# Bringing the second batch's first head pair forward into the first batch's last, with its loads between smaller groups of weight columns

## The chip, the cores and the metric

The kernel runs on one core of a Trainium2 chip. The metric is device time in microseconds (us), lower is better. The median of the kernel before is 318.94 us over its first three runs (318.9 to 319.49). The runs of the kernel before spread by 0.2% to 1.2% within one batch (318.9 to 319.49 us in the first, 316.93 to 320.62 in the last), and its medians moved from 318.9 to 319.7 us between batches, so every experiment below is read by its ratio to runs of the kernel before on the same chip in the same rounds.

Names: PE is the matmul engine (TensorE), PEld its weight load, DVE is VectorE, ACT is ScalarE, POOL is GpSimd, SP issues most loads. PSUM holds the tiles that PE writes in the traces below (psTk, psGT, psS, psH). T(4) and S(4,0) stand for what `emit_T(4)` and `emit_S(4, 0)` make.

## The reference, cut to what matters

Eight batches, eight heads of width 64, 512 local and 32 global positions. The attention output goes through a gated feed-forward product.

```python
# local queries see 32 neighbours on each side and all 32 global keys
# global queries see everything; softmax over each row
x = attn_out.transpose(0, 2, 1, 3).reshape(B * S, H * D)     # 8 * 544 rows of 512
h = x @ w_in                                                 # 512 -> 2048
g = h * np.clip(h + 3.0, 0.0, 6.0) / 6.0
out = g @ w_out                                              # 2048 -> 512
```

## The kernel before

The work is cut into 32 head pairs, four to a batch. Pairs 0 to 3 are batch 0, pairs 4 to 7 batch 1. For each pair `emit_T` transposes k and q on PE, `emit_S` makes two halves of the scores and their exponentials, `emit_AV` multiplies by v, and `emit_X` transposes the result for the feed-forward product. `u1(c)` makes one block of 128 of the 2048 columns of `x @ w_in`, in four matmuls (one for each pair of the batch), followed by one activation on ScalarE and one gate product on VectorE. In the traces below each engine makes its matmuls, copies and activations in the order in which the program emits them (on ScalarE in the kernel before: the casts of w_in 4 to 7 end at 24.47 us, the activations of the first seven blocks start at 24.63, the copy of qT(4) at 28.64, the exponentials of S(4,0) at 31.69; PE's and VectorE's timelines are below).

```python
def load_w(kind, i):            # one 256 KB tile of w_in, float32, into a staging buffer
    nc.sync.dma_start(out=t, in_=moe_w_in[m * P:(m + 1) * P, qd * 512:(qd + 1) * 512])
def cast_w(kind, i, eng):       # to float16, on the engine that is given
    (eng.copy if eng is nc.scalar else eng.tensor_copy)(out=o, in_=w_st[kind, i])
...
def emit_T(p, qdve=False):
    ...                          # 8 transposes on PE
    nc.vector.tensor_copy(out=kv[...], in_=ps["k"]...)       # kT on VectorE, L229
    qcopy(out=qT[...], in_=ps["q"]...)                       # qT on ScalarE, L232
    ...                          # and its first 32 columns once more, L237
def cast_G(b0, b1, nm, eng=nc.vector):                       # global keys to float16, VectorE, L191
def emit_G(b0, b1, nm):          # transposes them on PE (L201), copies to kgT on VectorE (L209)
def kglob(b, eng):               # copies kgT into kT, L213; the second half of the scores reads it
def vglob(b, eng):               # copies the global values into vb, L147; 1.88 us on GpSimd
def emit_S(p, ch):
    ...                          # 2 matmuls that write the mask (L281), 8 of scores (L293),
    ...                          # 2 exponentials on ScalarE (L297)
def u1(c, ms=range(NM)):
    ...                          # 4 matmuls, L426
    nc.scalar.activation(out=t1[:, 0:n], in_=ps[:, 0:n], func=RELU, ...)          # L431
    nc.vector.scalar_tensor_tensor(out=gts[c][:, 0:n], in0=t1[:, 0:n], ...)       # L433
```

The order of compute around the seam between the batches:

```python
    emit_S(3, 1)
    for i in range(4, 8):
        cast_w("in", i, nc.scalar)          # four casts on ScalarE
    emit_X(1)
    emit_AV(2)
    HEAD = 4
    for c in range(HEAD):
        u1(c, range(2))                      # pairs 0 and 1 of the first four blocks
    emit_X(2)
    emit_AV(3)
    for c in range(HEAD):
        u1(c, range(2, 3))
    emit_X(3)
    for c in range(HEAD):
        u1(c, range(3, 4))
    u1(4)
    u1(5)
    u1(6)
    emit_T(4)
    cast_G(1, 4, "kg")
    emit_T(5)
    emit_G(1, 4, "kg")
    emit_S(4, 0)
    u1(7)
    kglob(1, nc.vector)
    u1(8)
    emit_S(4, 1)
    ...
```

The softmax here doesn't subtract the row's maximum and nothing guards it: scores larger than these inputs give would overflow.

Of the kernel before, what the change touches and what calls it, by code (L numbers as in the profile page):

```python
# [14 lines left out]
def kernel(  # L15
# [12 lines left out]
    nc = tc.nc  # L28
# [88 lines left out]
    def load(p, what="kqv"):  # L117
        b, m = divmod(p, NM)
        s = st.setdefault(p, {})
        for c in what:  # L120
            src = {"k": k_l, "q": q_l, "v": v_l}[c]
            t = stage()
            if c != "v" and b < NRUN:
                nc.sync.dma_start(out=t.rearrange("p (h x) -> p h x", h=2),  # L124
                                  in_=src[b, 2 * m:2 * m + 2].rearrange("h (p j) d -> p h (j d)", j=NT))
            else:
                nc.sync.dma_start(out=t.rearrange("p (h kb d) -> p (h kb) d", h=2, kb=NT),  # L127
                                  in_=src[b, 2 * m:2 * m + 2].rearrange("h (kb p) d -> p (h kb) d", p=P))
            s[c + "f"] = t.rearrange("p (h kb d) -> p kb h d", h=2, kb=NT)

    def cast(p, what, eng):
        b, m = divmod(p, NM)
        s = st[p]
        for c in what:
            if c == "v":
                o = vts[b % NV][:, :, m, vc].rearrange("p kb (h d) -> p kb h d", h=2)
            else:
                s[c + "n"] = wrk.tile([P, NT, P], FP16, tag=c + "n", name=c + "n", bufs=4)
                o = s[c + "n"].rearrange("p kb (h d) -> p kb h d", h=2)
            eng.tensor_copy(out=o, in_=s[c + "f"])  # L140
# [27 lines left out]
    def cast_w(kind, i, eng):  # L168
        if kind == "in":
            qd, m = divmod(i, NM)  # L170
            o = w_in_t[m][:, qd * 512:(qd + 1) * 512]
        else:
            o = w_out_t[i // 4][:, i % 4]
        (eng.copy if eng is nc.scalar else eng.tensor_copy)(out=o, in_=w_st[kind, i])  # L174
# [5 lines left out]
    def load_g(b0, b1, nm):  # L180
        src = {"kg": k_g, "qg": q_g}[nm]
        t = stage()
        nc.sync.dma_start(
            out=t[:, 0:(b1 - b0) * HH * D].rearrange("p (n d) -> p n d", d=D),
            in_=src[b0:b1].rearrange("b (x y) s d -> (y s) (b x) d", x=HH))
        gst[b0, nm] = t
# [29 lines left out]
    def emit_T(p, qdve=False):  # L216
        b, m = divmod(p, NM)
        s = st[p]
        kT = kTs[b % 2][:, m]
        kv = kT[:, 0:NT * KW].rearrange("p (u c) -> p u c", u=NT)  # L220
        qT = wrk.tile([P, Sl + W], FP16, tag="qT", name="qT", bufs=5)
        ps = {}
        for c in "kq":
            ps[c] = ps_tile("psT" + c, FP16)[:, 0:Sl]
            for j in range(NT):
                nc.tensor.matmul(out=ps[c][:, j * P:(j + 1) * P], lhsT=s[c + "n"][:, j], rhs=ident,
                                 is_transpose=True)
        qcopy = nc.vector.tensor_copy if qdve else nc.scalar.copy
        nc.vector.tensor_copy(  # L229
            out=kv[:, :, 0:P].rearrange("p u (i j) -> p u i j", j=NT),  # L230
            in_=ps["k"].rearrange("p (j u i) -> p u i j", j=NT, u=NT))
        qcopy(out=qT[:, W:Sl + W].rearrange("p (i j) -> p i j", j=NT),  # L232
              in_=ps["q"].rearrange("p (j i) -> p i j", j=NT))
        if b == 0:
            nc.vector.tensor_copy(out=qT[:, 0:W], in_=qT[:, Sl:Sl + W])
        else:
            nc.scalar.copy(out=qT[:, 0:W].rearrange("p (i j) -> p i j", j=NT),  # L237
                           in_=ps["q"].rearrange("p (j i) -> p i j", j=NT)[:, P - W // NT:P])
        s["qT"], s["kT"] = qT, kT
# [59 lines left out]
    def emit_S(p, ch):  # L299
        emit_Sm(p, ch)  # L300
        emit_Ss(p, ch)
# [22 lines left out]
    def emit_AV(p):  # L324
        b, m = divmod(p, NM)
        E = st[p]["E"]
        vt, vb = vts[b % NV], vbs[b % NV]
        xn = wrk.tile([P, NT, P], FP16, tag="xn", name="xn", bufs=3)
        st[p]["xn"] = xn
        for w2 in range(NT // 2):  # L330
            po = ps_tile("pav").rearrange("p (w c) -> p w c", w=2)
            for i in range(2):
                w = 2 * w2 + i
                for e in range(2):
                    o = po[:, i, e * (D + 1):(e + 1) * (D + 1)]
                    c = slice(1 + e * (D + 1), 1 + (e + 1) * (D + 1))
                    nc.tensor.matmul(out=o, lhsT=E[:, 0, e, w * P:(w + 1) * P],  # L337
                                     rhs=vt[:, w, m, c], start=True, stop=False,
                                     skip_group_check=True)
                    nc.tensor.matmul(out=o, lhsT=E[:, 1, e, w * P:(w + 1) * P],  # L340
                                     rhs=vb[:, (w - 1) % NT, m, c], start=False, stop=True,
                                     skip_group_check=True)
            rc = wrk.tile([P, 2, 2], FP32, tag="rc", name="rc", bufs=4)
            nc.vector.reciprocal(out=rc, in_=po[:, :, 0:2 * D + 2:2 * D + 1])
            nc.vector.tensor_tensor(  # L345
                out=xn[:, 2 * w2:2 * w2 + 2].rearrange("p w (e d) -> p w e d", e=2),
                in0=po[:, :, 1:1 + P].rearrange("p w (e d) -> p w e d", e=2),
                in1=rc.unsqueeze(3).to_broadcast([P, 2, 2, D]), op=mult)
# [38 lines left out]
    def emit_X(p):  # L387
        b, m = divmod(p, NM)
        xn = st[p]["xn"]
        if b > 3 or (b == 3 and m < NM - 1):  # L390
            xt = wrk.tile([P, Sl], FP16, tag=f"xt{m}", name=f"xt{m}", bufs=2)
            xts.setdefault(b, []).append(xt)
            nc.sync.dma_start_transpose(out=xt.rearrange("p (w c) -> p w c", w=NT),
                                        in_=xn.rearrange("p w c -> p (w c)"))
            return
        psX = ps_tile("psX", FP16)
        for w in range(NT):
            nc.tensor.matmul(out=psX[:, w * P:(w + 1) * P], lhsT=xn[:, w], rhs=ident,
                             is_transpose=True)
        xt = wrk.tile([P, Sl], FP16, tag=f"xt{m}", name=f"xt{m}", bufs=2)  # L400
        xts.setdefault(b, []).append(xt)
        nc.vector.tensor_copy(out=xt, in_=psX[:, 0:Sl])
# [88 lines left out]
    load(3, "kq")  # L491
    for p in range(1, NM):
        load(p, "v")
    for i in range(8):
        load_w("in", i)
    load(4, "kq")
    load_g(1, 4, "kg")
    load(5, "kq")
    for i in range(8, 12):
        load_w("in", i)  # L500
    load(6, "kq")
    load(4, "v")
    load(5, "v")
    load(7, "kq")
    for i in range(12, NC):
# [41 lines left out]
    def ones_v(i, eng):  # L547
        for c in (1, 2 + P):
            eng.memset(vbs[i][0:P - W, :, :, c:c + 1], 1.0)
            eng.memset(vts[i][:, :, :, c:c + 1], 1.0)  # L550
# [16 lines left out]
    def first(p, what="kqv"):  # L567
        cast(p, what, nc.gpsimd)
        vshift(p, nc.gpsimd)
# [6 lines left out]
        first(p, "v")  # L576
    for i in range(4):
        cast_w("in", i, nc.gpsimd)
    ones_v(1, nc.gpsimd)
    vglob(1, nc.gpsimd)  # L580
    cast(4, "kq", nc.gpsimd)
    cast(5, "kq", nc.gpsimd)
    for i in range(8, 12):
        cast_w("in", i, nc.gpsimd)
    cast(6, "kq", nc.gpsimd)
    first(4, "v")
    first(5, "v")
    cast(7, "kq", nc.gpsimd)
    for i in range(12, NC):
# [37 lines left out]
        cast_w("in", i, nc.scalar)  # L627
    emit_X(1)
    emit_AV(2)
    HEAD = 4  # L630
    for c in range(HEAD):
        u1(c, range(2))
    emit_X(2)
    emit_AV(3)
    for c in range(HEAD):
        u1(c, range(2, 3))
    emit_X(3)
    for c in range(HEAD):
        u1(c, range(3, 4))
    u1(4)  # L640
    u1(5)
    u1(6)
    emit_T(4)
    cast_G(1, 4, "kg")
    emit_T(5)
    emit_G(1, 4, "kg")
    emit_S(4, 0)
    u1(7)
    kglob(1, nc.vector)
    u1(8)  # L650
    emit_S(4, 1)
    emit_T(6)
    u1(9)
    emit_S(5, 0)
    emit_AV(4)
    u1(10)
    emit_S(5, 1)
    emit_X(4)
    u1(11)
    emit_T(7)  # L660
    emit_S(6, 0)
    emit_AV(5)
    u1(12)
    emit_S(6, 1)
    emit_S(7, 0)
    emit_X(5)
    emit_AV(6)
    for t in Egs:
        nc.vector.memset(t[:, NT], 0.0)
    cast_G(0, 4, "qg")  # L670
    u1(13)
    emit_S(7, 1)
    emit_X(6)
    emit_G(0, 4, "qg")
    u1(14)
    emit_AV(7)
    u1(15)
    emit_SG(0)
    emit_SG(1)
    M(1)  # L680
    emit_TD(2 * NM)
    load(2 * NM + 1)
    cast(2 * NM + 1, "kq", nc.gpsimd)
# [1 line left out]
    emit_X(7)  # L685
    sum_E(0)
    sum_E(1)
    M(1)
    emit_SG(2)
    emit_SG(3)  # L690
    vglob(2, nc.gpsimd)
    kglob(2, nc.gpsimd)
    held = [units.pop(0), units.pop(0)]
    u2 = moe_units(lambda mm: xts[1][mm], Sl, local_dests(1))
    units[:0] = u2[0:NC]
# [143 lines left out]
```

## Time and profile before

| | kernel before |
|---|---|
| median of the first three runs | 318.94 us |
| span of the profiled run | 316.0 us |
| PE busy | 97% |
| PE idle, 18 us to 52.5 us | 3.80 us |
| granted PE clock in the profile | 1.00 |

The page of the profile: the span, the busy times, the granted clock in 40 slices, and the chain of waits followed back from the end, by engine.

```profile
span 316.0 us, 7320 instructions
...
PE 305.9 (97%) x2673; PEld 163.2 (52%) x2673; DVE 210.7 (67%) x485; ACT 200.6 (63%) x420; POOL 152.5 (48%) x270
...
PEclk9999999999999999999999999999999999999999
...
PE 79%; DVE 5%; DMA 5%; ACT 3%; SPq 3%; issue 2%; POOL 1%; POOLq 0%
```

The chain says PE. The 97% alone does not: a matmul of 512 columns is recorded as 379 ns, yet sixteen of them take 3.61 us, 216 ns apart after the first, because their records overlap. What is read here are PE's idle gaps. Here is PE's timeline; the columns are start, duration, engine, line, operation, and in brackets the idle time just before and what ended it.

```profile
19.33 0.39 PE L426 MATMUL psH<-xt,win 128*128 128x512 f16 x1 [0.79 <-POOL win L174]
...
24.22 3.61 PE L426 MATMUL psH<-xt,win 128*128 128x512 f16 x16 [0.52 <-DVE xt L402]
27.67 0.39 PE L226 MATMUL psTk<-ident,kn 128*128 128x128 f16 x4
...
30.55 0.34 PE L201 MATMUL psGT<-ident,kgn 128*128 128x128 f16 x3 [1.78 <-DVE kgn L191]
...
34.44 0.40 PE L293 MATMUL psS<-qT,kT 64*128 64x128 f16 x8 [0.52 <-DVE kT L213]
```

The largest gap, 1.78 us, waits for the cast of the global keys. VectorE's timeline shows why: the cast is short, but it stands behind seven gate products (and the copy of kT(4)).

```profile
25.35 4.27 DVE L433 SCALAR_TENSOR_TENSOR gt<-t,psH 128x512 f16<-128x512 f32 x7 [1.19 <-ACT t L431]
29.55 0.68 DVE L229 COPY kT<-psTk 128x512 f16<-128x512 f16 x1
30.15 0.35 DVE L191 CAST kgn<-stg 128x384 f16<-128x384 f32 x1
```

ScalarE, in the same stretch, casts w_in 4 to 7 as they land, and is done with it at 24.5 us, just when the first activations are ready:

```profile
23.17 1.30 ACT L174 CAST win<-stg 128x512 f16<-128x512 f32 x2 [0.73 <-DMA stg<-in_moe_w_in_dram]
24.63 4.16 ACT L431 ACTIVATE t<-psH,half_col 128x512 f32<-128x512 f32 x7 [0.16 <-PE psH L426]
```

### The profile page before, as it was taken

Reading aid. Unit: us, or ns where it says so; the run is one execution under the profiler, and the core shown is the slowest. Engines: PE = TensorE matmul, PEld = TensorE weight load, DVE = VectorE, ACT = ScalarE, POOL = GpSimd, SP = SyncE. Lnnn points to the kernel's source line nnn. Section 1 sums busy time; section 2 is a strip of 40 time slices with the busy share of each in tenths; the row PEclk is TensorE's granted clock in tenths of the full one; section 3 lists DMA queues with packets and bytes.
Section 4 is the critical chain, followed back from the end, with each engine's and each line's share of the span. In section 5 each row is a group of like instructions: output and inputs, shape, how many; then the busy total and the mean of one; then the engine's idle time right before and its main releaser. Section 6 shows DMA issues by size and latency. Waiting matters only on the chain.

```text
span 316.0 us, 7320 instructions
## 1 busy us (share of the span) xinstructions
PE 305.9 (97%) x2673; PEld 163.2 (52%) x2673; DVE 210.7 (67%) x485; ACT 200.6 (63%) x420; POOL 152.5 (48%) x270
## 2 busy tenths in 40 slices
PE   8887999999999999999999999999999999999995
PEld 5553455545555555555555554555555544448444
DVE  6758578897765799579845994468844962489101
ACT  6847887887443985479844993589556941579000
POOL 4876787599866565773686456443511000000000
PEclk9999999999999999999999999999999999999999
DMA  7999999999999799998999987886642002100131
GB/s 200 262 276 341 272 291 323 235 185 218 214 199 244 175 210 169 211 223 174 185 171 215 196 161 152 176 203 132 125 103 86 17 19 83 66 2 1 36 99 66
DMA packets 140260, 53.05 MB, mean 168 GB/s; under 512 B 127552, under 2 KB 131904, under 8 KB 140224
## 3 DMA queue, kind: packets, MB, share of 16 engines
q1 hardware_dynamic: 138048, 52.32, 75.5%
q0 software_dynamic: 2176, 0.26, 1.4%
q8 instruction: 21, 0.34, 0.5%
q14 instruction: 15, 0.12, 0.1%
HBM read 35.13 MB, written 8.91 MB: 139 GB/s over the span
## 4 chain that ended last, share of the span: by engine, by line
PE 79%; DVE 5%; DMA 5%; ACT 3%; SPq 3%; issue 2%; POOL 1%; POOLq 0%
PE po L442 34%; PE psH L426 31%; DMA stg<-in_v_l_dram 4%; PE psS L268 3%; DVE gt L433 2%; PE pav L337 2%; PE pav L340 2%; SPq L124 2%; DVE E L275 2%; PE psSG L311 1%; SPq L127 1%; ACT t L431 1%; DMA stg<-in_k_l_dram 1%; PE po L454 1%; ACT E L272 1%
## 5 line engine op out<-in xcount | busy, mean ns | idle before, releaser
L442 PE MATMUL po<-wout,gt 128*128 128x512 f16 x528 | 122.6, 379 | 0.0
L426 PE MATMUL psH<-xt,win 128*128 128x512 f16 x512 | 119.1, 379 | 1.7 <-POOL win L174 1.0
L433 DVE SCALAR_TENSOR_TENSOR gt<-t,psH 128x512 f16<-128x512 f32 (+1 forms) x144 | 90.5, 653 | 22.0 <-ACT t L431 21.3
L431 ACT ACTIVATE t<-psH,half_col 128x512 f32<-128x512 f32 (+1 forms) x144 | 91.6, 670 | 15.6 <-PE psH L426 14.2
L426 PEld LDWEIGHTS <-win 128*128 128x128 f16 x576 | 53.0, 98 | 53.2 <-POOL win L174 1.4
L442 PEld LDWEIGHTS <-gt 128*128 128x128 f16 x528 | 48.4, 98 | 51.9
L275 DVE TENSOR_TENSOR E<-E,mk 128x512 f16<-128x512 f16 x96 | 48.7, 543 | 31.5 <-ACT E L272 30.2
L272 ACT ACTIVATE E<-psS 128x512 f16<-128x512 f32 x96 | 49.8, 604 | 13.3 <-PE psS L268 13.2
L446 ACT COPY ot<-po 128x512 f32<-128x512 f32 x16 | 9.4, 586 | 59.3 <-PE po L442 53.5
L140 POOL CAST kn<-stg 128x512 f16<-128x512 f32 x31 | 19.5, 631 | 31.9 <-DMA stg<-in_k_l_dram 30.2
L363 POOL TENSOR_TENSOR s<-Eg 128x128 f32<-128x128 f16 x24 | 10.8, 448 | 37.4 <-ACT Eg L312 36.5
L446 DVE COPY ot<-po 128x512 f32<-128x512 f32 x17 | 11.7, 690 | 23.0 <-PE po L442 23.0
L345 DVE TENSOR_TENSOR xn<-pav,rc 128x256 f16<-128x256 f32 x64 | 25.6, 421 | 1.1
L140 POOL CAST qn<-stg 128x512 f16<-128x512 f32 x31 | 20.4, 659 | 12.0 <-DMA stg<-in_q_l_dram 11.8
L140 POOL CAST vt<-stg 128x512 f16<-128x512 f32 x32 | 20.9, 654 | 8.9 <-DMA stg<-in_v_l_dram 8.4
L144 POOL COPY vb<-vt 64x512 f16<-64x512 f16 x32 | 20.2, 630 | 2.0
L297 ACT ACTIVATE E<-psS 128x512 f16<-128x512 f32 x32 | 17.1, 608 | 4.8 <-PE psS L293 4.6
L337 PE MATMUL pav<-vt,E 128*128 128x65 f16 x256 | 20.0, 194 | 0.0
L340 PE MATMUL pav<-vb,E 128*128 128x65 f16 x256 | 20.0, 195 | 0.0
L337 PEld LDWEIGHTS <-E 128*128 128x128 f16 x256 | 17.8, 99 | 3.4
L340 PEld LDWEIGHTS <-E 128*128 128x128 f16 x256 | 16.9, 97 | 3.0
L268 PEld LDWEIGHTS <-kT 64*128 64x128 f16 x384 | 11.7, 94 | 9.8 <-issue 8.5
(93 smaller groups left out, 277.4 us busy)
## 6 DMA issues: line engine op xcount, KB each, us to landing
stg<-in_k_l_dram SPq DMA_DIRECT2D x32, 256.0 KB, 3.5
stg<-in_q_l_dram SPq DMA_DIRECT2D x32, 256.0 KB, 4.1
stg<-in_v_l_dram SPq DMA_DIRECT2D x32, 256.0 KB, 4.6
out_dram<-ot SPq DMA_DIRECT2D x23, 256.0 KB, 3.7
stg<-in_moe_w_in_dram SPq DMA_DIRECT2D x16, 256.0 KB, 5.7
stg<-in_moe_w_out_dram SPq DMA_DIRECT2D x16, 256.0 KB, 4.7
out_dram<-ot SPq DMA_DIRECT2D x8, 192.0 KB, 3.9
out_dram<-ot SPq DMA_DIRECT2D x16, 64.0 KB, 1.9
```

Source lines behind the costliest of these rows:

```text
L140: eng.tensor_copy(out=o, in_=s[c + "f"])
L268: nc.tensor.matmul(out=pss[2 * ch + e][:, w * P:(w + 1) * P], lhsT=kT[r, c0:c0 + P], rhs=qT[r, w * P:(w + 1) * P])
L272: nc.scalar.activation(out=E[:, ch, e], in_=pss[2 * ch + e], func=EXP, scale=qk_scale)
L275: nc.vector.tensor_tensor(out=E[:, ch, e], in0=E[:, ch, e], in1=mk[:, ch].rearrange("p w c -> p (w c)"), op=mult)
L337: nc.tensor.matmul(out=o, lhsT=E[:, 0, e, w * P:(w + 1) * P], rhs=vt[:, w, m, c], start=True, stop=False, skip_group_check=True)
L340: nc.tensor.matmul(out=o, lhsT=E[:, 1, e, w * P:(w + 1) * P], rhs=vb[:, (w - 1) % NT, m, c], start=False, stop=True, skip_group_check=True)
L345: nc.vector.tensor_tensor(out=xn[:, 2 * w2:2 * w2 + 2].rearrange("p w (e d) -> p w e d", e=2), in0=po[:, :, 1:1 + P].rearrange("p w (e d) ...
L426: nc.tensor.matmul(out=ps[:, 0:n], lhsT=w_in_t[m][:, c * P:(c + 1) * P], rhs=rhs(m), start=(m == 0), stop=(m == NM - 1), skip_group_check= ...
L431: nc.scalar.activation(out=t1[:, 0:n], in_=ps[:, 0:n], func=RELU, bias=half_col, scale=1.0 / 6.0)
L433: nc.vector.scalar_tensor_tensor(out=gts[c][:, 0:n], in0=t1[:, 0:n], scalar=1.0, in1=ps[:, 0:n], op0=amin, op1=mult)
L442: nc.tensor.matmul(out=po[t][:, 0:dm], lhsT=gts[c][:, t * P:(t + 1) * P], rhs=w_out_t[c // 4][:, c % 4], start=(c == 0), stop=(c == NC - 1))
L446: (nc.scalar.copy if t % 2 else nc.vector.tensor_copy)(out=ot, in_=po[t][:, 0:dm])
```

## The change

The intent is to fill PE's gaps between 24 and 35 us: pair 4 of the second batch is transposed, and its first scores made, while the first batch's last pair is finished. For this its k and q are loaded before w_in 4 to 7, and the group of column blocks that hold PSUM buffers meanwhile shrinks from four to three. (The later interleaving of pairs 5 to 7 with `u1(9)` to `u1(15)` moves one step earlier in the same way.)

```diff
-    for i in range(8):
+    for i in range(4):
         load_w("in", i)
     load(4, "kq")
     load_g(1, 4, "kg")
+    for i in range(4, 8):
+        load_w("in", i)
     load(5, "kq")
+    load(4, "v")
...
     for i in range(4):
         cast_w("in", i, nc.gpsimd)
+    cast(4, "kq", nc.gpsimd)
     ones_v(1, nc.gpsimd)
     vglob(1, nc.gpsimd)
-    cast(4, "kq", nc.gpsimd)
     cast(5, "kq", nc.gpsimd)
+    first(4, "v")
...
-    HEAD = 4
+    HEAD = 3
...
     emit_AV(3)
+    emit_T(4)
+    cast_G(1, 4, "kg")
     for c in range(HEAD):
         u1(c, range(2, 3))
     emit_X(3)
+    emit_G(1, 4, "kg")
+    emit_S(4, 0)
     for c in range(HEAD):
         u1(c, range(3, 4))
+    kglob(1, nc.vector)
+    u1(3)
+    emit_S(4, 1)
     u1(4)
+    emit_T(5)
     u1(5)
+    emit_S(5, 0)
     u1(6)
-    emit_T(4)
-    cast_G(1, 4, "kg")
...
```

No instruction is added or taken away.

More of the change, by code (lines that the diff above doesn't have):

```diff
@@ L501 @@
     load(6, "kq")
-    load(4, "v")
     load(5, "v")
@@ L585 @@
     cast(6, "kq", nc.gpsimd)
-    first(4, "v")
     first(5, "v")
@@ L637 @@
     emit_X(3)
+    emit_G(1, 4, "kg")
+    emit_S(4, 0)
     for c in range(HEAD):
         u1(c, range(3, 4))
+    kglob(1, nc.vector)
+    u1(3)
+    emit_S(4, 1)
     u1(4)
+    emit_T(5)
     u1(5)
+    emit_S(5, 0)
     u1(6)
-    emit_T(4)
-    cast_G(1, 4, "kg")
-    emit_T(5)
-    emit_G(1, 4, "kg")
-    emit_S(4, 0)
+    emit_S(5, 1)
+    emit_AV(4)
     u1(7)
-    kglob(1, nc.vector)
+    emit_T(6)
+    emit_X(4)
     u1(8)
-    emit_S(4, 1)
-    emit_T(6)
-    u1(9)
-    emit_S(5, 0)
-    emit_AV(4)
-    u1(10)
-    emit_S(5, 1)
-    emit_X(4)
-    u1(11)
-    emit_T(7)
     emit_S(6, 0)
     emit_AV(5)
-    u1(12)
+    u1(9)
     emit_S(6, 1)
+    emit_X(5)
+    emit_T(7)
+    u1(10)
     emit_S(7, 0)
-    emit_X(5)
     emit_AV(6)
@@ L670 @@
     cast_G(0, 4, "qg")
-    u1(13)
+    u1(11)
     emit_S(7, 1)
     emit_X(6)
+    u1(12)
     emit_G(0, 4, "qg")
-    u1(14)
     emit_AV(7)
-    u1(15)
+    u1(13)
     emit_SG(0)
     emit_SG(1)
-    M(1)
+    u1(14)
     emit_TD(2 * NM)
@@ L687 @@
     sum_E(1)
+    u1(15)
     M(1)
@@ L692 @@
     kglob(2, nc.gpsimd)
+    M(1)
     held = [units.pop(0), units.pop(0)]
```

## The prediction

> **What bounds the kernel.** TensorE. The summary gives PE 97% busy; the chain of waits is 79% PE (34% second MoE product, 31% first). The summed pieces of 35.2 to 49.8 us (seven first products at 0.86 us, six score halves at 0.87, four value products at 0.5, transposes) fill that stretch completely. So the change acts only through PE idle time before 36 us, which then reaches the end one for one. In the timeline of PE it is: 0.47 us (at 15.7), 0.79 and 0.17 (19.3 to 19.9, GpSimd's casts of w_in), 0.52 (24.2), 1.78 (28.7 to 30.55: the small key cast waits on VectorE behind seven gate products), 0.52 (34.4). The last three, 2.8 us, are what the change aims at.
>
> **What it moves.** No instruction is added or removed. Pair 4's k and q load ahead of w_in tiles 4 to 7; its transposes and first scores come ahead of the last products of the first group, which shrinks from four to three column blocks.
>
> **Costing.** Each load waits for the one eight places earlier, so issue times give landing times: w_in 3 at 20.5, then a 256 KB load each 0.65 to 0.85 us (w_in 7 about 23.8, k4 24.6, k_g 26.2). In the new order k4 lands about 21.1, q4 21.8, k_g 22.9, w_in 4 to 7 about 23.7, 24.4, 25.2, 26.1.
> - Gain: T(4) runs near 22 us instead of 27.7; the 1.78 us stall disappears.
> - Wait 1: PE reaches T(4) at 21.7; GpSimd's casts end 21.8 (k) and 22.5 (q): about 0.7 us lost.
> - Wait 2, the large one: on ScalarE the casts of w_in 4 to 7 (0.62 us each) still stand before the copy of qT(4). The last cast now ends about 26.7 instead of 24.5, the copy about 27.4. The order listing shows the first mask matmul of S(4) waiting on ScalarE too. PE has nothing else after about 24.3 and stands about 3 us.
> - Wait 3: then ScalarE holds two exponentials (1.0), four activations (0.6 each), two more exponentials and qT(5) before S(5) can start: 0.5 to 1 us more.
> [...]
>
> Idle between 19 and 36 us: about 3.8 before, 4.5 to 5.7 after. The wait moves rather than disappears: net +1.2 us, 0 to +2.5 likely.
>
> **Prediction: 320.1 us (before 318.94), range 317.9 to 322.0; faster by over 2%: 1%; within 2%: 97%; slower by over 2%: 2%.**
>
> **What would show each step.** Right: pair 4's k cast starts 21.1 to 21.5 us; ScalarE's four w_in casts spread out, each waiting for its load, the last ending 26 to 27; the copy of qT(4) follows at once; PE has one wait of 2 to 3.5 us just before S(4,0), released by ScalarE; the wait on the small key cast is gone; after 40 us PE is packed as before, the trace shifted by a constant of about 1 us. Wrong: the last w_in cast ends before 25.5, or PE's wait before S(4,0) is below 1.5 us; then the change gains 1 to 2 us.
>
> **What would make it wrong.** Loads landing faster than one per 0.75 us around 20 to 26 us; a PSUM buffer wait I don't see; later stretches (70 to 110 us) absorbing or amplifying the shift[...].

+1.2 us comes from PE's idle time alone (4.5 to 5.7 us after, about 3.8 before), and 318.94 + 1.2 gives 320.1. Wait 2 stands on the order seen on ScalarE in the kernel before (its times are given above). That each load waits for the one eight places earlier is read from the same trace: the loads issued at 17.25, 17.91, 18.56, 20.57, 21.21 and 21.86 us each follow the landing of that load by 0.06 to 0.07 us.

## More of the kernel before

Busy time in stretches of 2 us (columns: stretch, its length, busy PE, PEld, DVE, ACT, POOL with counts, granted clock, DMA share, GB/s). PE is idle for 1.23 us from 28 to 30, and the clock stays at 1.00.

```profile
26.00:28.00 2.00, 2.00 (x15) 1.05 (x14) 2.00 (x5) 2.00 (x4) 1.08 (x3) 1.00 1.04 366
28.00:30.00 2.00, 0.77 (x14) 0.55 (x10) 2.00 (x4) 1.93 (x6) 1.90 (x4) 1.00 1.06 366
```

## The result, and the profile after

| | before | changed |
|---|---|---|
| median (four runs each) | 319.02 us | 323.1 us |
| lowest to highest | 318.9 to 319.49 | 322.36 to 323.5 |
| ratio, 95% interval | | 1.0123 (1.0099 to 1.0146) |
| span of the profiled run | 316.0 us | 321.6 us |
| mean granted PE clock of the four runs | (profile: 1.00) | 0.989, 0.989, 0.995, 0.993 |

Ratios here and below are the mean time of one kernel's fast runs over that of the other's fast runs of the same rounds, so not quite the ratio of the medians. The change costs 4 us, and its median lies above the predicted range (317.9 to 322.0).

The page after. The clock row has a dip that the kernel before doesn't have (the fourth slice, 24 to 32 us).

```profile
span 321.6 us, 7314 instructions
...
PE 307.8 (96%) x2673; PEld 163.3 (51%) x2673; DVE 214.1 (67%) x485; ACT 201.3 (63%) x420; POOL 151.5 (47%) x270
...
PEclk9995999999999999999999999999999999999999
```

PE's timeline. The 1.78 us wait is gone, as intended. In its place stand four others, and the largest is the one before the first masks of pair 4 (L281), 2.73 us, released by ScalarE's copy of qT. (The masks don't read qT, only constants. What they wait for is probably the PSUM buffer that this copy empties; that was not tested. The scores behind them read qT anyway.)

```profile
21.95 0.40 PE L226 MATMUL psTk<-ident,kn 128*128 128x128 f16 x4 [1.41 <-POOL kn L140]
22.64 0.40 PE L226 MATMUL psTq<-ident,qn 128*128 128x128 f16 x4 [0.30 <-POOL qn L140]
...
25.13 0.34 PE L201 MATMUL psGT<-ident,kgn 128*128 128x128 f16 x3 [1.22 <-DVE kgn L191]
28.20 1.01 PE L281 MATMUL psS<-mneg,ident 128*128 128x512 f16 x2 [2.73 <-ACT qT L237]
...
33.72 0.40 PE L293 MATMUL psS<-qT,kT 64*128 64x128 f16 x8 [0.53 <-DVE kT L213]
```

ScalarE's timeline: the same four casts, each now waiting for its load, and the copy of qT behind them. The transposed q had been in PSUM since 23.0 us.

```profile
23.34 1.32 ACT L174 CAST win<-stg 128x512 f16<-128x512 f32 x2 [5.05 <-DMA stg<-in_moe_w_in_dram]
25.20 0.62 ACT L174 CAST win<-stg 128x512 f16<-128x512 f32 x1 [0.53 <-DMA stg<-in_moe_w_in_dram]
26.95 0.62 ACT L174 CAST win<-stg 128x512 f16<-128x512 f32 x1 [1.14 <-DMA stg<-in_moe_w_in_dram]
27.48 0.58 ACT L232 COPY qT<-psTq 128x512 f16<-128x512 f16 x1
```

VectorE's timeline: the cast of the global keys, 0.35 us before, takes 2.08 us; and kT's global part (L213) comes only after three gate products that wait for ScalarE.

```profile
22.99 2.08 DVE L191 CAST kgn<-stg 128x384 f16<-128x384 f32 x1
...
31.54 1.88 DVE L433 SCALAR_TENSOR_TENSOR gt<-t,psH 128x512 f16<-128x512 f32 x3 [4.97 <-ACT t L431]
33.34 0.33 DVE L213 COPY kT<-kgT 128x512 f16<-128x512 f16 x1
```

GpSimd's timeline has the long copy that runs beside that cast:

```profile
22.97 1.88 POOL L147 COPY vb<-vg 32x2048 f16<-32x2048 f16 x1
```

The stretches of 2 us (columns as before). PE does nothing from 26 to 28 us; from there to 32 us it works, but at half its clock: seven matmuls take 3.08 us from 29.68 us, where they take 1.68 us at full clock in the first experiment below. The trace's clock record falls to 0.50 at 25.72 us, only 0.25 us into the wait of 2.73 us (25.47 to 28.20), and is back at 1.00 at 32.55. So nearly all of that long wait came after the fall. In the 3.4 us before it (as long as one spell of low clock in e1, e2 and e9 below) PE had been idle for 1.77 us, most of it the wait of 1.22 us.

```profile
24.00:26.00 2.00, 0.34 (x3) 0.23 (x4) 1.88 (x4) 1.24 (x2) 0.85 (x1) 0.93 1.08 352
26.00:28.00 2.00, 0.00 (x0) 0.00 (x0) 0.54 (x3) 1.04 (x3) 0.24 (x1) 0.50 1.12 321
28.00:30.00 2.00, 1.80 (x11) 0.58 (x11) 0.00 (x0) 0.31 (x3) 1.59 (x3) 0.50 1.03 324
30.00:32.00 2.00, 2.00 (x6) 0.76 (x5) 0.47 (x1) 2.00 (x5) 1.93 (x4) 0.50 1.05 322
```

**Where the 5.6 us between the two profiles are.** A mark that both kernels reach with the same work behind them is PE's first pair of column blocks of the second batch (8 matmuls in a row): 52.52 us before, 58.16 us after. PE's timeline, before and then changed:

```profile
52.52 1.89 PE L426 MATMUL psH<-xt,win 128*128 128x512 f16 x8
```

```profile
58.16 1.89 PE L426 MATMUL psH<-xt,win 128*128 128x512 f16 x8
```

From the mark to the end both take the same, 263.48 and 263.44 us. So all of it arises before. Up to the mark I add PE's idle time, and an estimate of the work lost to the low clock (busy time times one minus the granted clock, in stretches of 0.2 us):

| 18 us to the mark | before | changed | difference |
|---|---|---|---|
| PE idle | 3.80 | 7.49 | +3.69 |
| lost to the low clock | 0.00 | 2.17 | +2.17 |
| sum | 3.80 | 9.66 | +5.86 |

Up to 18 us the idle times are 2.21 and 2.17 us. The sum accounts for the 5.64 us of the marks within 0.2. The medians differ by less, 4.1 us, because the profiled run of before was a quick one: its span is 316.0 us, and eleven other runs of it in the first batch of experiments span 316.6 to 318.4.

### The profile page after: what moved, and what is told of

Its sections match the earlier page's. It is cut to its first block, busy times and chain, and to the rows that moved or that the text cites. A ratio compares the mean times of both kernels' runs of the same rounds, so it can differ in the third digit from the quotient of the medians.

```text
span 321.6 us, 7314 instructions
## 1 busy us (share of the span) xinstructions
PE 307.8 (96%) x2673; PEld 163.3 (51%) x2673; DVE 214.1 (67%) x485; ACT 201.3 (63%) x420; POOL 151.5 (47%) x270
## 4 chain that ended last, share of the span: by engine, by line
PE 73%; DVE 7%; DMA 6%; ACT 4%; POOL 4%; issue 2%; SPq 2%; POOLq 0%; ACTq 0%
PE psH L426 31%; PE po L442 28%; DVE gt L433 3%; PE psS L268 3%; DMA stg<-in_q_l_dram 3%; DMA stg<-in_moe_w_in_dram 2%; PE pav L337 2%; PE pav L340 2%; ACT t L431 2%; PE psS L293 2%; DVE xn L345 1%; PE psS L281 1%; DMA stg<-in_v_l_dram 1%; ACT E L272 1%; PE po L454 1%
## 5 line engine op out<-in xcount | busy, mean ns | idle before, releaser
L426 PE MATMUL psH<-xt,win 128*128 128x512 f16 x512 | 121.2, 383 | 0.5 <-DVE gt L433 0.4
L275 DVE TENSOR_TENSOR E<-E,mk 128x512 f16<-128x512 f16 x96 | 50.5, 563 | 32.0 <-ACT E L272 30.8
L140 POOL CAST vt<-stg 128x512 f16<-128x512 f32 x32 | 21.6, 674 | 7.0 <-DMA stg<-in_v_l_dram 6.4
```

Source lines behind the costliest of these rows:

```text
L140: eng.tensor_copy(out=o, in_=s[c + "f"])
L275: nc.vector.tensor_tensor(out=E[:, ch, e], in0=E[:, ch, e], in1=mk[:, ch].rearrange("p w c -> p (w c)"), op=mult)
L426: nc.tensor.matmul(out=ps[:, 0:n], lhsT=w_in_t[m][:, c * P:(c + 1) * P], rhs=rhs(m), start=(m == 0), stop=(m == NM - 1), skip_group_check= ...
```

## The experiments

Theory A, as first stated: the copy of qT(4) behind four casts on ScalarE makes the long wait, and the wait drops the clock (the clock record above, at 0.50 from 0.25 us into that wait, already speaks against the second half of it). Rival B: the later order of compute costs by itself. The first experiment forced a second version, A2: there are several waits for copies that stand behind work emitted earlier on the same engine, one behind the other, and taking one away exposes the next. Each experiment starts from the changed kernel unless said otherwise. All results were correct.

| run | median us | ratio to before, 95% interval | PE idle / lost to clock, 18 us to the mark |
|---|---|---|---|
| changed kernel | 323.1 | 1.0123 (1.0099, 1.0146) | 7.49 / 2.17 |
| e1 casts later on ScalarE | 322.92 | 1.0101 (1.0086, 1.0116) | 6.41 / 1.64 |
| e2 dummies in two gaps | 323.41 | 1.0123 (1.0101, 1.0144) | 4.60 / 1.71 |
| e3 long copy moved | 322.26 | 1.0087 (1.0072, 1.0102) | 6.96 / 1.70 |
| e4 loads only | 321.71 | 1.0062 (1.0040, 1.0083) | 4.55 / 1.71 |
| e5 order only | 324.21 | 1.0134 (1.0103, 1.0164) | 6.76 / 1.71 |
| e6 casts on GpSimd and two more | 318.0 | 0.9945 (0.9920, 0.9970) | 3.52 / 0 |
| e7 a milder version from before | 319.83 | 0.9997 (0.9974, 1.0021) | 4.05 / 0 |
| e8 dummies in all gaps | 321.94 | 1.0065 (1.0042, 1.0089) | 2.63 / 0 |
| e9 casts on GpSimd alone | 320.59 | 1.0047 (1.0011, 1.0083) | 5.01 / 1.71 |
| e10 like e6, casts on ScalarE | 320.21 | 1.0044 (1.0006, 1.0082) | 4.13 / 1.43 |
| e11 e6 with pair 5 earlier | 318.15 | 0.9979 (0.9946, 1.0013) | 3.98 / 0 |
| e12 e6 with the long copy back | 318.87 | 1.0005 (0.9966, 1.0044) | 3.85 / 0 |

The last column is of the one profiled run, and loads land at different times in different runs: the last of the moved loads, w_in 7, landed between 25.26 us (e12) and 26.93 us (changed kernel) in the profiles with this order of loads, and at 27.59 in e4, which had started late. In e2 and e8 the dummies count as busy, so their idle time is not comparable. The kernel before had medians of 319.55, 319.73 and 318.89 us in the three batches (e1 to e4, e5 to e8, e9 to e12), and in the last it scattered most (316.93 to 320.62), so ratios within 0.3% of each other across batches should not be ranked.

### e1: the casts after the first exponentials

```diff
-    for i in range(4, 8):
-        cast_w("in", i, nc.scalar)
     emit_X(1)
...
     emit_S(4, 0)
+    for i in range(4, 8):
+        cast_w("in", i, nc.scalar)
```

> The changed kernel, with ScalarE's four casts of w_in 4 to 7 placed after the first two exponentials of pair 4 instead of before the copy of qT(4). Theory A (the queue on ScalarE makes the long wait, and the wait lets the clock drop): the 2.7 us wait on the copy of qT(4) is gone or below 0.5 us, the granted clock is 1.00 in every 2 us stretch from 20 to 40 us, and the time falls by 3 to 5 us from the changed kernel's 323.1, to 318 to 320. Rival B (the loss comes mainly from the later order on PE, VectorE and ScalarE, after 33 us, or from loads): the wait goes but the time stays within 1.5 us of 323.

Measured: 1.0101, a miss. The wait before S(4,0) is gone, and PE makes the first scores at 24.4 us. Then it stands 4.12 us before the second half. PE's timeline of e1:

```profile
30.95 0.61 PE L293 MATMUL psS<-qT,kT 64*128 64x128 f16 x8 [4.12 <-DVE kT L213]
```

ScalarE's timeline, and VectorE's, show the chain behind it:

```profile
25.84 2.17 ACT L174 CAST win<-stg 128x512 f16<-128x512 f32 x4
27.91 2.43 ACT L431 ACTIVATE t<-psH,half_col 128x512 f32<-128x512 f32 x4
```

```profile
28.64 1.88 DVE L433 SCALAR_TENSOR_TENSOR gt<-t,psH 128x512 f16<-128x512 f32 x3 [3.36 <-ACT t L431]
30.44 0.45 DVE L213 COPY kT<-kgT 128x512 f16<-128x512 f16 x1
```

The casts now hold back the activations, these the gates, and the copy of the global keys into kT stands behind the gates on VectorE, though its input is ready at 25.3 us. The second half of the scores reads it. So Theory A named a real wait, but not the only one: the wait moved by one step. The time is the one that was written down for B (within 1.5 us of 323), but B isn't confirmed as it was written there, since the loss is still at 27 to 31 us, not later. The clock fell to 0.50 from 30.8 to 34.2 us.

### e2: dummy matmuls in two gaps

```diff
+    warm_up(8)
     emit_G(1, 4, "kg")
+    warm_up(20)
     emit_S(4, 0)
```

> The changed kernel with dummy matmuls in the two idle places before the first scores of pair 4 (8 of 256 columns before the transposes of the global keys, 20 before the scores; about 0.11 us each at full clock, so about 3 us in 4 us of idle). The wait stays, only the clock should stay up. If the halved clock (28.2 to 32.3 us at 0.50) costs what the trace suggests: granted clock 1.00 throughout, time 1.5 to 2.5 us below the changed kernel, 320.5 to 321.8. If the clock record costs nothing beyond the wait: 323 as before. If the dummies overrun the idle: the time gains less, and PE shows no wait there.

Measured: 1.0123, a miss. The 20 dummies take 2.38 us, so 0.11 to 0.12 us each, as was estimated, and the clock is 1.00 where they stand. The next wait is 1.93 us before S(4,1), for the same copy as in e1, and the clock is at 0.50 behind it, from 32.8 to 36.2 us. So the median doesn't tell what the clock costs; e8 does better. The six runs differ among themselves, though: two had a mean clock of 1.00 and took 322.7 us on average, the four with 0.993 to 0.995 took 323.8. So the clock fell in some runs of one kernel and not in others.

### e3: GpSimd's long copy out of the way

```diff
-    ones_v(1, nc.gpsimd)
-    vglob(1, nc.gpsimd)
     cast(5, "kq", nc.gpsimd)
+    ones_v(1, nc.gpsimd)
+    vglob(1, nc.gpsimd)
```

> The changed kernel with GpSimd's copy of the global values of batch 1 (1.88 us) moved behind the casts of pair 5, so that it no longer runs beside VectorE's cast of the global keys, which took 2.08 us beside it against 0.35 us in the kernel before. If the two engines shut each other out: the cast takes 0.35 us again, and PE's wait for it falls from 1.22 us to under 0.3. Theory A says that this wait hides under the longer one for the copy of qT(4), which then grows by as much: the time stays within 1 us of 323.1. The rival (the blocked cast is a cost of its own) says 1 to 1.5 us less.

Measured: the cast takes 0.35 us, PE's wait for it vanishes, and the wait for qT(4) grows from 2.73 to 3.48 us. PE's timeline:

```profile
27.55 0.59 PE L281 MATMUL psS<-mneg,ident 128*128 128x512 f16 x2 [3.48 <-ACT qT L237]
```

So in the trace the blocked cast hid under the longer wait. The times don't settle it. The median, 322.26 us, is within the us that was expected; but the ratio, 1.0087 against 1.0123, is 1.1 us lower, which is what the rival said, and the two intervals overlap. A part of it may be the clock: this profile has one spell of low clock (28.7 to 32.1 us), the changed kernel's two in a row.

The cast and the copy did shut each other out. In the changed kernel GpSimd started 0.02 us earlier, and the cast ended 0.22 us after GpSimd's copy. In the profiles of e1, e2 and e8, with the same two instructions, VectorE started first, the cast took 0.35 us, and GpSimd's copy was the one that stretched (2.06, 1.98, 2.05 us against 1.88). In these four profiles the one that started first took its usual time, and the other was stretched; what lies behind it was not shown. VectorE was 0.04 us earlier in e1 and 0.05 in e8, so one profile is no proof that this collision is always, or never, there.

### e4: the new loads with the old compute

From the kernel before: only the load order and GpSimd's order of the changed kernel.

> The kernel before, with only the new order of loads and of GpSimd's work (pair 4's k and q, the global keys, then w_in 4 to 7). PE, VectorE and ScalarE keep the order of before. The casts of w_in 4 to 7 then end near 27 us instead of 24.5, and stand ahead of the activations of the first group: PE waits for a free PSUM buffer or for w_in 7 near 25.3 us. Theory A: most of the loss comes from here, 1.5 to 3 us over before (320.5 to 322). Rival B (the new order of compute is what costs): within 0.7 us of before.

Measured: 1.0062, inside what A expected, though not quite as it said. The two waits for w_in on PE are 0.31 and 0.32 us. The rest comes through ScalarE: its seven activations start at 28.14 us instead of 24.63, the gates follow, and the cast of the global keys is later still. PE's timeline:

```profile
34.21 0.34 PE L201 MATMUL psGT<-ident,kgn 128*128 128x128 f16 x3 [2.44 <-DVE kgn L191]
```

The clock then falls (35.1 to 38.5 us). This profile also lost 1.71 us to a low clock before 18 us, which the changed kernel's did not.

### e5: the new compute with the old loads

> The changed kernel's order of compute with the loads and GpSimd's order of before, the other half of the change. k4 then lands near 24.6 us while PE asks for it near 20.4: a wait of 4 to 5 us at T(4), after which the clock is halved for one or two spells of 3.4 us. The casts of w_in are done by 24.6 us and no longer stand before qT(4). Theory A2 (both halves of the change lose by themselves: the earlier transposes want loads that can't be there, the later w_in wants ScalarE; each costs about 2 us of PE idle or more plus a spell of low clock): 321.5 to 323.5. Rival (only the loads' order costs, as the run with the loads alone at +0.6% might suggest): within 0.3% of before.

Measured: 1.0134. k and q of pair 4 aren't there, as expected, though PE waits 3.25 us for them and not 4 to 5; the time is 0.7 us above the expected range. PE's timeline:

```profile
25.34 0.40 PE L226 MATMUL psTk<-ident,kn 128*128 128x128 f16 x4 [3.25 <-POOL kn L140]
```

The clock is at 0.50 for one spell of 3.4 us (26.5 to 29.9), as long as those of e1 and e2, from which the expectation has its figure. After the wait at T(4) comes another of 1.86 us before S(4,1) for kT's global part, although ScalarE's casts are over by then. Both halves of the change lose by themselves, 0.6% and 1.3%, so Rival B as worded at the head of this section is a part of the answer. Together they cost 1.2%, less than the sum: the new loads shorten the wait at T(4) from 3.25 to 1.41 us, and pay for it at the copy of qT(4).

### e6: three things out of the queues

```diff
-    for i in range(4, 8):
-        cast_w("in", i, nc.scalar)
...
     cast(4, "kq", nc.gpsimd)
+    for i in range(4, 8):
+        cast_w("in", i, nc.gpsimd)
+    cast(5, "kq", nc.gpsimd)
     ones_v(1, nc.gpsimd)
     vglob(1, nc.gpsimd)
-    cast(5, "kq", nc.gpsimd)
...
     emit_G(1, 4, "kg")
+    kglob(1, nc.vector)
     emit_S(4, 0)
...
-    kglob(1, nc.vector)
     u1(3)
```

> The changed kernel with three waits behind other work in a queue taken away: w_in 4 to 7 are cast by GpSimd in its idle time (not by ScalarE ahead of qT(4) and the activations), the copy of the global keys into kT stands before the gate products on VectorE (it was what the second score half waited for, 4.1 us, when only the casts were moved), and GpSimd's long copy of global values comes after the casts of pair 5. Theory A2: the waits before S(4,0) and S(4,1) fall under 0.7 us each; what stays is the wait for k4 and q4 (1.5 to 2 us) and one for w_in 7 before the fourth column block (0.3 to 1.5 us)[...]. Granted clock 1.00. Time 318.5 to 320.5, about the time of before and 3 us under the changed kernel. Rival (the loss sits in the later part, 34 us on): above 321.5.

Measured: 318.0 us against 319.73 for the kernel before in the same rounds, ratio 0.9945 with an interval that excludes 1. This is faster than both kernels in this batch, and 0.5 us better than the expected range. (The gain over the kernel before rests on this one batch of six runs: e11 and e12 in the next batch, which differ from it in one place each, show none. The two profiles differ by 0.3 us at the mark, 52.21 against 52.52.) The four casts run on GpSimd from 23.32 to 26.13 us, where in the changed kernel it has nothing to do from 24.85 to 27.75. No wait is left before S(4,0), S(4,1) or the fifth column block, and the clock stays at 1.00. The waits over 0.3 us that remain in PE's timeline from 18 to 40 us are:

```profile
21.85 0.40 PE L226 MATMUL psTk<-ident,kn 128*128 128x128 f16 x4 [1.03 <-POOL kn L140]
22.63 0.40 PE L226 MATMUL psTq<-ident,qn 128*128 128x128 f16 x4 [0.38 <-POOL qn L140]
...
31.24 0.40 PE L293 MATMUL psS<-qT,kT 64*128 64x128 f16 x8 [1.24 <-DVE kT L229]
```

### e7: a milder version from the kernel before

From the kernel before, with its loads:

```diff
     u1(4)
-    u1(5)
-    u1(6)
     emit_T(4)
     cast_G(1, 4, "kg")
+    u1(5)
+    u1(6)
     emit_T(5)
+    u1(7)
     emit_G(1, 4, "kg")
     emit_S(4, 0)
-    u1(7)
```

> The kernel before, loads untouched, with pair 4 brought forward only as far as its loads allow: its transposes after the first column block of the second group instead of the third, the cast of the global keys with them (so on VectorE it stands behind five gate products, not seven), and their transposes after the fourth block. Should remove the 1.78 us wait on the global keys' cast and the 0.52 us wait at 34.4: 1 to 2.3 us less than before, 0.3 to 0.7% faster (ratio 0.993 to 0.997), with no wait over 0.8 us from 25 to 36 us. If it isn't faster, PE's idle time before 36 us does not reach the end one for one.

Measured: 0.9997, a miss. The 1.78 us wait is gone. But shorter ones came (0.36, 0.67, 0.35, and 0.84 us before S(4,1)), and in this run PE waits near 50 us for w_out, matmul by matmul, which the profile of before does not show:

```profile
50.83 0.38 PE L442 MATMUL po<-wout,gt 128*128 128x512 f16 x1 [0.18 <-POOL wout L174]
51.38 0.38 PE L442 MATMUL po<-wout,gt 128*128 128x512 f16 x1 [0.18 <-POOL wout L174]
```

GpSimd starts the w_out casts at 49.05 us instead of 45.84, after waiting 1.59 and 1.42 us for earlier loads. So PE's idle time before 36 us does not always reach the end one for one, as the prediction had it: there is a second limit near 50 us. Whether the edit delayed the loads, or whether this profile had a slow start of its own, isn't settled by one profile.

### e8: dummies in all gaps

Dummy matmuls as in e2, and 8 before `emit_T(4)` and 12 before `emit_S(4, 1)`.

> The changed kernel with dummy matmuls in all of its idle places (8 before T(4), 8 before the global keys, 20 before S(4,0), 12 before S(4,1); about 5 us of dummies), so that the clock stays at 1.00. The earlier run with only two places filled kept the clock up there, but the next wait (1.93 us) dropped it for a spell of 3.4 us. If the low clock costs what was added up from the trace (2.2 us of lost work in the changed kernel): 320.8 to 321.8 with clock 1.00. If the clock stays up and the time stays at 323, the low clock hides under other waits and costs nothing of its own.

Measured: mean clock 0.998 to 1.00 in all six runs, 321.94 us, ratio 1.0065 against the changed kernel's 1.0123, with intervals that do not overlap. The median is 0.14 us above the expected range (320.8 to 321.8); the ratio, taken to the 319.02 us of the first batch, gives 321.1, inside it. Two of the stretches of 2 us (columns as before), where the changed kernel has a clock of 0.50:

```profile
26.00:28.00 2.00, 2.00 (x23) 1.34 (x20) 0.21 (x1) 0.90 (x3) 0.81 (x2) 1.00 1.15 327
28.00:30.00 2.00, 2.00 (x16) 1.10 (x13) 0.12 (x1) 1.81 (x4) 1.47 (x3) 1.00 1.01 351
```

The waits themselves are still there, filled with dummies, so the low clock costs about 0.58%, 1.9 us; from the trace it was 2.17. Two other things differ between the two profiles, so neither figure is exact: in e8 VectorE's cast of the global keys started before GpSimd's copy and took 0.35 us, not 2.08, and w_in 7 landed at 25.68 us, not 26.93. The runs of one kernel among themselves agree in size for a single spell: those with a mean clock of 0.993 to 0.995 are slower than those with 0.999 or 1.00 by 1.1 us in e2, 1.45 in e9 and 1.3 in e12 (two to four runs on each side).

### e9: only the casts moved to GpSimd

```diff
-    for i in range(4, 8):
-        cast_w("in", i, nc.scalar)
...
     vglob(1, nc.gpsimd)
+    for i in range(4, 8):
+        cast_w("in", i, nc.gpsimd)
     cast(5, "kq", nc.gpsimd)
```

> The changed kernel with only the casts of w_in 4 to 7 moved from ScalarE to GpSimd (after its copy of global values); the copy of the global keys into kT stays behind the gate products on VectorE. Theory A2: the wait before S(4,0) on qT(4) is gone; the wait before S(4,1) on the global keys in kT appears, 1 to 2.5 us, since three activations and gates have to run first; after it perhaps a spell of low clock. Time between the version with all three taken away (ratio 0.9945) and the changed kernel (1.0123): ratio 0.998 to 1.006. If the casts alone were the cause, the ratio is 0.9945 as well.

Measured: 1.0047, as expected. The wait for qT(4) is gone, and the next one stands as A2 says, followed by a spell of low clock from 29.9 to 33.3 us:

```profile
29.77 0.53 PE L293 MATMUL psS<-qT,kT 64*128 64x128 f16 x8 [2.29 <-DVE kT L213]
```

### e10: e6 with the casts on ScalarE

As e6, but the four casts on ScalarE after `emit_S(4, 0)`.

> The casts of w_in 4 to 7 stay on ScalarE but come after the first two exponentials of pair 4; the global keys go into kT ahead of the gates; GpSimd's long copy comes after the casts of pair 5. Differs from the best run so far only in which engine casts w_in 4 to 7. Theory A2: no wait before S(4,0) or S(4,1); the 2.2 to 2.5 us of casts on ScalarE then push four activations, two exponentials and qT(5) back, so PE waits 2 to 3 us before S(5,0), where the best run waited 1.24. Ratio 1.000 to 1.006. Rival (ScalarE has room once the order is right): ratio 0.993 to 0.997.

Measured: 1.0044, as expected in size, but the wait isn't where I put it. ScalarE's backlog holds the activations, so the gates come late, so PSUM buffers come free late, and PE waits for one before pair 5's transposes:

```profile
29.18 0.38 PE L226 MATMUL psTk<-ident,kn 128*128 128x128 f16 x4 [0.92 <-DVE gt L433]
```

With the smaller ones after it (0.21, 0.22, 0.55 us) this is 1.9 us. With the casts on ScalarE (2.17 us) its activations start at 27.71 us, with the casts on GpSimd (e6) at 25.89: ScalarE has no room for them in this stretch, GpSimd does.

### e11: e6 with pair 5 earlier

```diff
-    u1(4)
     emit_T(5)
+    u1(4)
     u1(5)
     emit_S(5, 0)
```

> The best run so far (casts on GpSimd, global keys early, long copy late), with pair 5's transposes ahead of the fifth column block, so that the copy of kT(5) on VectorE and of qT(5) on ScalarE stand one gate and one activation earlier. Should take away its 1.24 us wait before S(5,0) at a price of 0.3 us waiting for q5: 0.5 to 1.0 us less, ratio to before 0.991 to 0.994. If the ratio stays at 0.9945, something later (the w_out casts near 50 us) has become the limit.

Measured: 0.9979, a miss. The interval (0.9946 to 1.0013) includes 1 and ends just above e6's 0.9945: no gain shown. The 1.24 us wait before S(5,0) is gone. In its place PE waits 0.90 and 0.43 us for GpSimd's casts of k5 and q5, which start as soon as their loads let them (k5 landed at 27.04 us, its cast started at 27.16): at this point the loads are the limit. PE also waits 0.44 us for pair 6's cast, and that is GpSimd's own queue: k6 had landed at 32.46 us, and its cast started at 34.51, behind four casts of w_in. The other explanation that was written down, the w_out casts, doesn't hold: PE shows no wait for w_out in this profile.

### e12: e6 with the long copy back

> The best run so far with GpSimd's long copy of global values put back where the changed kernel has it, beside VectorE's cast of the global keys. If GpSimd starts first, the cast takes about 2 us instead of 0.35 (as in the changed kernel) and now nothing hides it: PE waits 1.2 us before the global keys' transposes, and kT's first scores follow later: 0.5 to 1.5 us slower than the best run, ratio 0.996 to 0.999. If VectorE starts first (as in the run with dummies in two places), the cast takes 0.35 us and the ratio stays near 0.9945.

Measured: GpSimd started first (22.60 us), the cast took 1.75 us (22.94 us), and PE waited for it:

```profile
24.75 0.34 PE L201 MATMUL psGT<-ident,kgn 128*128 128x128 f16 x3 [1.22 <-DVE kgn L191]
```

The ratio is 1.0005, a little above the expected 0.996 to 0.999, against e11's 0.9979 in the same rounds. So the wait for the blocked cast, hidden in the changed kernel's trace, is exposed in the good version. The direction and the trace fit, but the intervals overlap, and e11 also has pair 5's transposes earlier, so the size (about 0.8 us by these means) is not settled.

## Why the prediction was wrong

The waits were foreseen, in their places and with their causes, and so was the sign. In the sum that was made of them two terms were too small and one, the clock, was left out.

1. **"Pair 4's k cast starts 21.1 to 21.5 us; … the copy of qT(4) follows at once; PE has one wait of 2 to 3.5 us just before S(4,0), released by ScalarE; the wait on the small key cast is gone."** The cast started at 21.28 us, the last w_in cast ended at 27.57 (predicted 26 to 27, so 0.6 us late), the copy followed, and the wait was 2.73 us. This part held, except that the wait on the small key cast did not disappear: it was 1.22 us instead of 1.78, because the cast took 2.08 us beside GpSimd's copy, which I hadn't considered. In e3's trace it hid under the next wait; by e3's times it cost between nothing and about 1 us.
2. **"Wait 1: … about 0.7 us lost."** It was 1.41 and 0.30 us. The casts ended when predicted; PE came to T(4) earlier, because its first column blocks started at 18.06 us in this run and 19.33 in the other. A wait for something that arrives at a fixed time grows when the waiter gets there sooner, and this part of the loss is no extra time.
3. **"PE … stands about 3 us."** 1.22 and 2.73 us, 3.95 together. w_in 7 landed about 0.8 us later than worked out from the loads of before (26.93 against 26.1). That is largely this run: in the profiles with the same order of loads it landed between 25.26 and 26.93 us, e4 with its late start apart.
4. **"Wait 3: … 0.5 to 1 us more."** After 28.2 us the waits are 0.53, 0.36, 0.42 and 0.26 us, 1.6 in all.
5. **"Net +1.2 us, 0 to +2.5 likely" is the step that failed.** It summed idle time only, as about 3.8 us before and 4.5 to 5.7 after, between 19 and 36 us; the profiles have 3.35 and 6.18 us there, 2.8 more, and 3.69 more up to the mark. And it left out the clock. The low clock stood in the last paragraph only as a risk, outside the sum and the range. It happened: the profile has it from 25.7 to 32.5 us, beginning after waits of 1.41, 0.30 and 1.22 us, all four runs have a mean clock of 0.989 to 0.995, and it cost 2.17 us by the trace and 1.9 us by e8. (The mean alone doesn't show this. Of the 33 runs of the kernel before in the experiments 15 have a mean clock of 0.993 to 0.995 too, and are only 0.4 us slower on average than the other 18, 319.59 against 319.17. No profile here shows where the low clock fell in those, so the smaller difference is not explained.) With that cost added the prediction's 320.1 us would have been 322.0 to 322.3, still about 1 us short.

Wait 2 takes it that ScalarE does its work in the order in which it was emitted, as in the trace of before. The runs agree (in the changed kernel the transposed q was there at 23.0 us, and its copy started at 27.48, behind the last cast), but I applied it to one queue. That on VectorE, too, the copy into kT stands behind gates that wait for ScalarE was visible in the order of the instructions, and e1 and e9 show that it costs 4.12 and 2.29 us when the first wait is gone.

What stays open: how much of the changed kernel's time is the collision of the cast with GpSimd's copy, which went one way with starts 0.02 us apart and the other way with 0.04; e7's late w_out; whether e6 really gains on the kernel before; and whether the early copy into kT alone, with the casts left on ScalarE where the change has them, would help.

## What to carry to other kernels

When work is brought forward, follow every engine's queue from the new place, not only PE's: here the copy that feeds the early work stood behind what was emitted before it on its engine (PE waited 2.73 us for it), and that was casts waiting for loads which the same change had moved later. Taking the first such wait away showed the next (ScalarE, 2.73 us; then VectorE, 4.12 in e1; then PSUM, 0.92 in e10; then the loads and GpSimd's queue, 0.90 and 0.44 in e11), so move all of them off that chain together: the changed order no longer loses (0.9945 in e6, 0.9979 in e11) once the casts run on an engine that is idle there. Price PE's idle time with the low clock that may follow it, here one or two spells of 3.4 us at half speed, and add up short waits: in these profiles PE had been idle for 1.5 to 3.4 us of the 3.4 us before a spell, while stretches with up to 1.8 us (the kernel before, e12) passed without one. The waits just before a spell were 1.41, 0.30 and 1.22 us and the first 0.25 us of the next (changed kernel), 1.93 us (e2), 2.29 us (e9), and 0.92, 0.21 and 0.22 us (e10, a spell from 31.0 to 34.4 us). The spells were 3.4 us long in e1, e2, e9 and e10, and 6.8 us (25.7 to 32.5) in the changed kernel.
